# Attention beside a GELU layer on one core: the row maxima turned by VectorE's block transposition, their float16 parts made by GpSimd

## The chip, the cores and the metric

The kernel runs on one core of one Trainium2 chip. The core has five engines that run side by side, each with an instruction queue worked in order: TensorE (PE; PEld is its weight load), VectorE (DVE), ScalarE (ACT), GpSimd (POOL) and SyncE (SP). SP does no arithmetic here; it issues every transfer of the part that this text is about. TensorE writes its products to PSUM, eight banks of 128 partitions by 512 float32 numbers; the other memory of the core is SBUF. The metric is the device time of one execution in microseconds (us); less is better.

## The reference

One input x of 2048 rows and 512 columns goes through a layer normalization, and then through two branches whose results are added to x: attention with 32 heads of 16 numbers each, and a two-layer network with 1792 hidden numbers.

```python
def reference(A_x, A_wqkv, A_wo, B_x, B_w1, B_b1, B_w2, B_b2):
    def _A_ref(x, wqkv, wo):
        B, S, D = x.shape          # 1, 2048, 512
        H = 32
        Dh = D // H                # 16
        qkv = (lambda x, *d: x.transpose(*d))((x @ wqkv).reshape(B, S, 3, H, Dh), 2, 0, 3, 1, 4)
        q, k, v = qkv[0], qkv[1], qkv[2]
        scores = jnp.einsum("bhqd,bhkd->bhqk", q, k) * (Dh ** -0.5)
        p = _softmax(scores, axis=-1)
        o = jnp.einsum("bhqk,bhkd->bhqd", p, v)
        return (lambda x, *d: x.transpose(*d))(o, 0, 2, 1, 3).reshape(B, S, D) @ wo

    def _B_ref(x, w1, b1, w2, b2):
        h = _gelu(jnp.einsum("bsd,df->bsf", x, w1) + b1)
        return jnp.einsum("bsf,fd->bsd", h, w2) + b2

    x = A_x
    xn = _layernorm(x, axis=-1)
    return x + _A_ref(xn, A_wqkv, A_wo) + _B_ref(xn, B_w1, B_b1, B_w2, B_b2)
```

## The kernel before, in words

**Tiles and units.** Heads are taken in groups g of four (NG = 8), queries in blocks qb of 512 (NQB = 4). One group with one block is a tile t, 32 tiles in all. A tile has 16 units; a unit u = 16 t + i is 128 queries against 512 keys for the scores, and, later, 128 keys against 512 queries for the exponentials. So there are NU = 512 units.

**What a unit does.** The function `unit` writes out, for unit u, four score products (`s_half`, one for each head of the group): TensorE puts 128x512 scores into a bank pS, and VectorE takes their row maxima (`reduce_max`, line 259) into the tile mt. Between them stand the four exponentials (`e_half`) of unit e = u - 20 (LEAD = 20): TensorE computes the scores again, with keys on the partitions, into a bank pT, and ScalarE takes their exponentials into pe (line 304). After each two of these come products with the values (pV, `v_half`) of units e - 1 and e - 2, and some products of the dense work (pD: projections, the two-layer network), which fill TensorE. Nearly all products go through the helper at line 170, in four pieces of 32 columns.

**What becomes of the maxima.** The exponentials need the maximum of each query subtracted. That is done inside the product: the tiles kst and qst hold, for each head, 48 rows of float16 parts of keys and queries, and in rows 62 and 63 ones (kst) and the negative maxima (qst), as a high and a low float16 part. After unit 15 of a tile, `s_end` reduces mt to mneg (line 270, 128 queries in the partitions, 16 columns for head and query block, of 32 that the tile has). Then `store` turns mneg so that the queries lie along a row: TensorE multiplies it with the unit matrix into a bank pS (line 277, two products), VectorE makes the two parts mhl out of that bank (lines 280 and 281), SP writes mhl to the HBM tensor m_d (line 284, two transfers) and from there into rows 62 and 63 of the four heads of qst (line 289, four transfers, which wait until the writes have landed). The exponentials of that tile start with unit 20 after its first unit, which is the fifth unit (number 4, counted from 0) after the tile's last one.

**PSUM.** The banks are handed out in turn: three to scores (`banks("S")`), three to exponentials, one to the dense work, one to pV. A score product waits until VectorE has read the bank's last content, which is that of the score product three before it, or of `store`, which takes its bank from the same turn.

**Order.** All five engines follow the order in which the program is written out. `later(n, fn)` puts a function off by n ticks; `tick`, at the end of each unit, runs those that are due. `store` is put off by `later(1, ...)` from the end of the tile's last unit, so it is written out at the end of the next unit (number 0 of the next tile). GpSimd's larger steps wait in a list (`pooled`), of which each tick releases as many as fit an estimate of 2500 ns.

**Other steps that are named below.** `v_end` divides a tile's result by its sums: ScalarE copies it to osb, SP sends the sums through HBM (lines 342, 345, 352, 356), VectorE inverts them (dn, line 348), GpSimd multiplies and splits (osb and ot, lines 360 to 362). hh, t and g are stages of the GELU on GpSimd (lines 992 to 1022), xa and yt its summed result (lines 1033 to 1049), wc and xb weights and inputs that SP fetches (lines 565 and 560).

Of the kernel before, what the change touches and what calls it, by code (L numbers as in the profile page):

```python
# [8 lines left out]
F32 = mybir.dt.float32  # L9
F16 = mybir.dt.float16  # L10
I32 = mybir.dt.int32
AF = mybir.ActivationFunctionType
ALU = mybir.AluOpType
# [4 lines left out]
P = 128  # L18
S = 2048
# [24 lines left out]
MROW = 1024.0  # L44
# [4 lines left out]
def layer_kernel(ctx: ExitStack, tc: tile.TileContext, x, wqkv, wo, w1, b1, w2, b2, out):  # L49
    nc = tc.nc  # L50
# [3 lines left out]
    def pool(stack, name, bufs=1, space=None, side=None):  # L54
        kw = {k: v for k, v in (("space", space), ("side", side)) if v is not None}
        return stack.enter_context(tc.tile_pool(name=name, bufs=bufs, **kw))

    const = pool(ctx, "const")
    work = pool(ctx, "work")
# [9 lines left out]
    m_d = dram.tile([NG * NQB, 16, 2, P], F16, name="m_d")  # L69
# [4 lines left out]
    ident = const.tile([P, P], F32, name="ident")  # L74
# [30 lines left out]
    def bank_tile(k, tag):  # L105
        return ps.tile([P, QB], F32, tag=f"B{k}", bufs=1, name="p" + tag)

    def banks(tag):
        k = free_banks[tag].pop(0)
        free_banks[tag].append(k)  # L110
        return bank_tile(k, tag)
# [48 lines left out]
    def given(engine, ns):  # L160
        backlog[engine] += ns
# [32 lines left out]
    def tiled(user, dst, lhs, rhs, start, stop):  # L194

        for j in range(0, P, 32):
            product(user, dst[j:j + 32], lhs[:, j:j + 32], rhs, start=start, stop=stop)
# [15 lines left out]
    def later(n, fn, local=False):  # L213
        queue.append((slot[0] + n, fn, local))
# [25 lines left out]
    def flush():  # L240

        while steps or any(q[2] for q in queue):
            run_due()
            run_steps(True)
            slot[0] += 1

    def s_half(u, n):

        t, i = divmod(u, 16)
        g, qb = divmod(t, NQB)  # L250
        qt, kb = divmod(i, 4) if t else (i % 4, i // 4)
        if t not in mt_of:
            mt_of[t] = work.tile([P, 4, 4, 4], F32, name="mt", bufs=2)
        ks, qs = kst[g % 2], qst[g % 2]
        p, a = divmod(n, 2)
        r = slice(64 * a, 64 * a + 62)
        s = banks("S")
        tiled(None, s, qs[p][qb][r, qt * P:(qt + 1) * P], ks[p][kb][r, :], True, True)
        nc.vector.reduce_max(mt_of[t][:, n, qt, kb:kb + 1], s, axis=AX.X)  # L259
        given("dve", 600)  # L260

    def s_end(u):

        t, i = divmod(u, 16)
        if i < 15:
            return
        g, qb = divmod(t, NQB)
        qs = qst[g % 2]
        mneg = mnegs[t % 2]
        nc.vector.tensor_reduce(mneg[:, :16], mt_of[t].rearrange("p h t k -> p (h t) k"), axis=AX.X, op=ALU.max, negate=True)  # L270
        given("dve", 220)

        def store():

            pt = banks("S")
            for a in range(2):
                nc.tensor.matmul(pt[32 * a:32 * a + 32, :64], mneg[64 * a:64 * a + 64, :],
                                 ident[64 * a:64 * a + 64, 64 * a:64 * a + 64], start=True, stop=True)
            mhl = work.tile([64, 2, 64], F16, name="mhl", bufs=2)
            nc.vector.tensor_scalar_mul(mhl[:, 0], pt[:64, :64], 1.0 / MROW)  # L280
            nc.vector.scalar_tensor_tensor(mhl[:, 1], pt[:64, :64], 1.0 / MROW, mhl[:, 0], op0=ALU.mult, op1=ALU.subtract)
            given("dve", 300)
            for a in range(2):
                nc.sync.dma_start(m_d[t, :, :, 64 * a:64 * a + 64], mhl[32 * a:32 * a + 16])
            for p in range(2):
                for a in range(2):
                    h = 2 * p + a
                    dst = qs[p][qb][64 * a + 62:64 * a + 64, :].rearrange("r (t q) -> r t q", q=P)
                    nc.sync.dma_start(dst, m_d[t, 4 * h:4 * h + 4].rearrange("t r q -> r t q"))

        later(1, store)

    def e_half(u, n):

# [101 lines left out]
    NU = NG * NQB * 16  # L396
# [215 lines left out]
    def unit(gen):  # L612
# [7 lines left out]
        for a in range(2):  # L620
            for scores, n in ((0, 1), (1, 0), (1, 1), (0, 0)) if a == 0 else ((1, 2), (0, 3), (0, 2), (1, 3)):
                if scores and u < NU:
                    s_half(u, n)
                elif not scores and 0 <= e < NU:
                    e_half(e, n)
            if e >= 0:
                enter()

                w, r = (e - 2, 1) if a == 0 else (e - 1, 0)
                live = 0 <= w < NU  # L630
                new = r == 0 and w % 16 == 0
                dense(gen, 1 - r, lambda: v_half(w, r) if live and not new else None)
                if live and new:
                    v_half(w, r)

                for user, goes_on in (("V", live and not (r == 1 and w % 16 == 15)),
                                      ("D", cur[0] is not None and not cur[0].over())):
                    leave(user, goes_on)
                for k in backlog:
                    backlog[k] = max(0, backlog[k] - HALF)  # L640
                if live and r == 1:
                    v_end(w)
                ended()
        if u < NU:
            s_end(u)
# [12 lines left out]
    with ExitStack() as st1:  # L658
# [130 lines left out]
        def tile_and_unit(t):  # L789

            v = v_proj(t, wvh, vbank)
            for k in range(2):
                s_half(t, 2 * k)
                s_half(t, 2 * k + 1)
                some(v, 6)
            s_end(t)
            run(v)
# [409 lines left out]
```

## Time and profile before

| what | value |
|---|---|
| time, median of 3 runs (lowest to highest) | 1502.55 us (1499.8 to 1506.8) |
| the profiled execution: its own time, and its span | 1504.39 us, 1502.6 us |
| PE busy | 1471.0 us (98%) |
| DVE busy | 1374.5 us (91%) |
| ACT busy | 1231.7 us (82%) |
| POOL busy | 716.6 us (48%) |
| mean granted TensorE clock | 0.994 |

The span runs from the first to the last instruction that the profiler recorded; the execution's own time has some 1.8 us around it. A busy PE is not PE at its peak, since its instructions overlap: its 98% says that nearly always a product was under way, not that none could have come sooner. In a row of a timeline the first number is the start in us from the beginning of the span, the second the time from the first to the last of the instructions that the row puts together (xN says how many), and the square bracket, where there is one, the idle time before and what ended it.

### The profile page before, as it was taken

Reading aid. Unit: us, or ns where it says so; the run is one execution under the profiler, and the core shown is the slowest. Engines: PE = TensorE matmul, PEld = TensorE weight load, DVE = VectorE, ACT = ScalarE, POOL = GpSimd, SP = SyncE. Lnnn points to the kernel's source line nnn. Section 1 sums busy time; section 2 is a strip of 40 time slices with the busy share of each in tenths; the row PEclk is TensorE's granted clock in tenths of the full one; section 3 lists DMA queues with packets and bytes.
Section 4 is the critical chain, followed back from the end, with each engine's and each line's share of the span. In section 5 each row is a group of like instructions: output and inputs, shape, how many; then the busy total and the mean of one; then the engine's idle time right before and its main releaser. Section 6 shows DMA issues by size and latency. Waiting matters only on the chain.

```text
span 1502.6 us, 87920 instructions
## 1 busy us (share of the span) xinstructions
PE 1471.0 (98%) x39971; PEld 931.1 (62%) x39971; DVE 1374.5 (91%) x2372; ACT 1231.7 (82%) x2326; POOL 716.6 (48%) x750
## 2 busy tenths in 40 slices
PE   8998999999999999999999999999999999999997
PEld 4434566666666666666666666666666666666653
DVE  7898989999999999999999999999999999999612
ACT  5315878899999889989998998998899999988771
POOL 4113597547665545537553554665264465511000
PEclk9999999999999999999999999999999999999998
DMA  6454476633211311121112211121112111022412
GB/s 207 129 172 139 160 217 221 196 116 94 71 37 44 89 43 37 36 68 54 36 51 59 63 37 37 35 83 57 37 43 63 53 32 35 23 68 81 152 35 89
DMA packets 113677, 123.82 MB, mean 82 GB/s; under 512 B 24988, under 2 KB 85276, under 8 KB 113304
## 3 DMA queue, kind: packets, MB, share of 16 engines
q1 hardware_dynamic: 113304, 118.21, 25.5%
q8 instruction: 312, 5.11, 1.4%
q14 instruction: 61, 0.50, 0.1%
HBM read 80.61 MB, written 37.34 MB: 78 GB/s over the span
## 4 chain that ended last, share of the span: by engine, by line
PE 81%; DVE 13%; DMA 2%; issue 2%; SPq 1%; ACT 1%; POOL 0%; ACTq 0%; POOLq 0%
PE pV L170 22%; PE pD L170 20%; PE pS L170 19%; PE pT L170 17%; DVE mt L259 11%; PE pT L444 1%; PE pS L444 1%; DVE amx L679 1%; PE pT L543 1%; PE pD L444 1%; DMA m_d<-mhl 1%; PE pV L543 0%; SPq L1080 0%; DMA xs<-in_A_x_dram 0%; DVE mneg L270 0%
## 5 line engine op out<-in xcount | busy, mean ns | idle before, releaser
L259 DVE TENSOR_REDUCE mt<-pS 128x1 f32<-128x512 f32 x2048 | 1274.3, 683 | 37.4 <-PE pS L170 22.4
L304 ACT ACTIVATE pe<-pT 128x512 f32<-128x512 f32 x2048 | 1107.0, 600 | 153.3 <-PE pT L170 79.2
L170 PE MATMUL pV<-pe,vv 64*32 64x512 f32 x8192 | 1093.1, 599 | 1.1 <-issue 1.0
L170 PE MATMUL pT<-qst,kst 64*32 64x512 f16 x8192 | 668.5, 377 | 3.5 <-ACT pe L304 1.8
L170 PE MATMUL pS<-kst,qst 62*32 62x512 f16 x8192 | 632.7, 379 | 8.7 <-DVE mt L259 6.1
L170 PE MATMUL pD<-xb,wc 64*32 64x512 f16 x5376 | 372.1, 375 | 0.0
L170 PE MATMUL pD<-w_s,g 64*32 64x512 f16 (+1 forms) x6144 | 362.0, 348 | 0.0
L170 PEld LDWEIGHTS <-qst 62*32 62x32 f16 x8192 | 248.1, 92 | 140.6 <-issue 49.5
L170 PEld LDWEIGHTS <-kst 64*32 64x32 f16 x8192 | 251.8, 93 | 101.4 <-issue 13.9
L170 PEld LDWEIGHTS <-g 64*32 64x32 f16 x6144 | 196.1, 92 | 85.3 <-issue 0.7
L170 PEld LDWEIGHTS <-wc 64*32 64x32 f16 x5376 | 177.4, 91 | 98.4
L170 PEld LDWEIGHTS pV<-pe,vv 64*32 64x32 f32 x8192 | 172.5, 105 | 6.0 <-issue 2.2
L1022 POOL TENSOR_SCALAR hh<-hh,fac,b_s 128x512 f32<-128x512 f32 x56 | 43.0, 768 | 265.3 <-ACT hh L1020 265.3
L170 PE MATMUL pD<-xt,wqk_h 64*32 64x512 f16 x1920 | 129.8, 377 | 3.1 <-issue 3.0
L360 POOL TENSOR_TENSOR osb<-osb,rb 128x512 f32<-128x512 f32 x31 | 39.8, 1283 | 140.1 <-DMA rb<-den_d 101.9
L1049 POOL TENSOR_TENSOR xa<-xa,yt 128x512 f32<-128x512 f32 x32 | 41.1, 1283 | 108.4 <-ACT yt L1047 108.4
L170 PEld LDWEIGHTS <-wqk_h 64*32 64x32 f16 x1920 | 61.8, 92 | 27.7 <-issue 3.6
L1086 DVE SCALAR_TENSOR_TENSOR ac<-pS,gs,ac 128x512 f32<-128x512 f32 x20 | 15.0, 751 | 66.1 <-PE pS L170 57.2
L993 POOL TENSOR_TENSOR t<-t,hh 128x512 f32<-128x512 f32 x56 | 71.8, 1283 | 4.7
L1000 POOL TENSOR_TENSOR t<-t,hh 128x512 f32<-128x512 f32 x56 | 71.7, 1281 | 4.7
L995 POOL TENSOR_TENSOR g<-t,g 128x512 f16<-128x512 f32 x56 | 65.2, 1164 | 4.7
L170 PE MATMUL pS<-wo_s,oc 64*32 64x512 f16 x1008 | 62.6, 377 | 0.4
(140 smaller groups left out, 926.3 us busy)
## 6 DMA issues: line engine op xcount, KB each, us to landing
wch<-in_B_w_dram SPq DMA_DIRECT2D x28, 512.0 KB
wc<-w_d SPq DMA_DIRECT2D x56, 256.0 KB
qk_d<-stg SPq DMA_DIRECT2D x32, 256.0 KB
rb<-den_d SPq DMA_DIRECT2D x124, 64.0 KB
w_d<-wsp SPq DMA_DIRECT2D x28, 256.0 KB
kst<-qk_d SPq DMA_DIRECT2D x128, 48.0 KB
qst<-qk_d SPq DMA_DIRECT2D x128, 48.0 KB
xs<-in_A_x_dram SPq DMA_DIRECT2D x16, 256.0 KB
```

Source lines behind the costliest of these rows:

```text
L170: p = nc.tensor.matmul(*args, **kw)
L259: nc.vector.reduce_max(mt_of[t][:, n, qt, kb:kb + 1], s, axis=AX.X)
L304: nc.scalar.activation(pe, st, AF.Exp, scale=factor(exp_scale, sexp[0:1, g // 2:g // 2 + 1]))
L360: pooled((1280, lambda: nc.gpsimd.tensor_tensor(osb, osb, rb, op=ALU.mult)), (620, lambda: nc.gpsimd.tensor_scalar(ot[:, 0], osb, 1.0, 0.0 ...
L444: nc.tensor.matmul(self.bank, lhs, rhs, start=start, stop=self.last and self.over())
L543: nc.tensor.matmul(pj, xt[:, i, c, t * P:(t + 1) * P], wh[j][:, c, :], start=(n == 0), stop=(n == 11))
L679: nc.vector.tensor_reduce(dst, v, axis=AX.XY if len(v.shape) == 3 else AX.X, op=ALU.max, apply_absolute_value=True)
L993: (1280, lambda: nc.gpsimd.tensor_tensor(t1, t1, hh, op=ALU.mult)),
L995: (1160, lambda: nc.gpsimd.tensor_tensor(g[:, 1, f, :], t1, g[:, 0, f, :], op=ALU.subtract)),
L1000: (1280, lambda: nc.gpsimd.tensor_tensor(t1, t1, hh, op=ALU.mult)),
L1022: later(1, lambda: pooled((690, lambda: nc.gpsimd.tensor_scalar(hh, hh, scale, bias, op0=ALU.mult, op1=ALU.add)), (0, lambda: gelu(hh, g, ...
L1049: add = lambda: nc.gpsimd.tensor_tensor(xa, xa, yt, op=ALU.add)
```

## The change

The transposition on TensorE goes, and with it the bank that it took and VectorE's two instructions that read this bank. In their place, VectorE transposes mneg in blocks of 32x32, in SBUF, into a new tile mrow of 128x32 (so block a holds queries 32 a to 32 a + 31, its rows 0 to 15 the head and query block). This is written out inside the next unit, right after that unit's first maximum; for the last tile at once. GpSimd then scales mrow in place and makes the two parts of mhl, in three instructions that stand outside the `pooled` list. SP writes mhl in four transfers (16 partitions x 2 parts x 32 numbers each) instead of two (16 x 2 x 64); the four transfers into qst are as before.

```diff
+    rows = []
     def s_half(u, n):
...
         nc.vector.reduce_max(mt_of[t][:, n, qt, kb:kb + 1], s, axis=AX.X)
         given("dve", 600)
+        if rows:
+            rows.pop()()
 
     def s_end(u):
...
+        pt = work.tile([P, 32], F32, name="mrow", bufs=2)
         def store():
-            pt = banks("S")
-            for a in range(2):
-                nc.tensor.matmul(pt[32 * a:32 * a + 32, :64], mneg[64 * a:64 * a + 64, :],
-                                 ident[64 * a:64 * a + 64, 64 * a:64 * a + 64], start=True, stop=True)
-            mhl = work.tile([64, 2, 64], F16, name="mhl", bufs=2)
-            nc.vector.tensor_scalar_mul(mhl[:, 0], pt[:64, :64], 1.0 / MROW)
-            nc.vector.scalar_tensor_tensor(mhl[:, 1], pt[:64, :64], 1.0 / MROW, mhl[:, 0], op0=ALU.mult, op1=ALU.subtract)
-            given("dve", 300)
-            for a in range(2):
-                nc.sync.dma_start(m_d[t, :, :, 64 * a:64 * a + 64], mhl[32 * a:32 * a + 16])
+            nc.vector.transpose(pt, mneg)
+            given("dve", 130)
+            mhl = work.tile([P, 2, 32], F16, name="mhl", bufs=2)
+            nc.gpsimd.tensor_scalar(pt, pt, 1.0 / MROW, 0.0, op0=ALU.mult, op1=ALU.add)
+            nc.gpsimd.tensor_scalar(mhl[:, 0], pt, 1.0, 0.0, op0=ALU.mult, op1=ALU.add)
+            nc.gpsimd.tensor_tensor(mhl[:, 1], pt, mhl[:, 0], op=ALU.subtract)
+            later(0, lambda: put(mhl))
+
+        def put(mhl):
+            for a in range(4):
+                nc.sync.dma_start(m_d[t, :, :, 32 * a:32 * a + 32], mhl[32 * a:32 * a + 16])
...
-        later(1, store)
+        rows.append(store)
+        if u == NU - 1:
+            rows.pop()()
```

How the instructions move is shown at the end of one tile in the middle of the program (tile 14 for PE and DVE). On PE, in the order at the beginning of unit 1 of the next tile (the difference; pT is a bank for exponentials, pD one of the dense work):

```order
 L170 LDWEIGHTS wc
 L170 MATMUL pD<-xb,wc 32x512
-L277 MATMUL pS<-ident,mneg_118 32x64 x2
 L170 LDWEIGHTS kst_0_3_92
 L170 MATMUL pT<-qst_0_1_106,kst_0_3_92 32x512
```

The two products with the unit matrix are gone; nothing else moved there.

On DVE, before, from the last maxima of tile 14 on (a trailing xN counts equal rows; the next tile's RECIPROCAL belongs to `v_end`):

```order
L259 TENSOR_REDUCE mt<-pS 128x1 [waits PE_49] x16
L270 TENSOR_REDUCE mneg_118<-mt 128x16 [waits DVE_49]
L259 TENSOR_REDUCE mt<-pS 128x1 [waits PE_49] x4
L280 TENSOR_SCALAR mhl<-pS 64x64 [waits DMAHW2_49,PE_49]
L281 SCALAR_TENSOR_TENSOR mhl<-pS,mhl 64x64 [waits DVE_49]
L259 TENSOR_REDUCE mt<-pS 128x1 [waits PE_49] x44
L348 RECIPROCAL dn<-dn 64x32 [waits DMAHW3_49,DMAHW1_49]
```

and now (the lines of the changed file are some ten higher):

```order
L261 TENSOR_REDUCE mt<-pS 128x1 [waits PE_49] x16
L274 TENSOR_REDUCE mneg_118<-mt 128x16 [waits DVE_49]
L261 TENSOR_REDUCE mt<-pS 128x1 [waits PE_49]
L281 STREAM_TRANSPOSE mrow<-mneg_118 128x32 [waits DVE_49,Pool_49]
L261 TENSOR_REDUCE mt<-pS 128x1 [waits PE_49] x47
L357 RECIPROCAL dn<-dn 64x32 [waits DMAHW7_49]
```

Two instructions after the fourth maximum of unit 0 became one after the first, and it no longer waits for PE.

On SP, at the end of tile 6, before:

```order
L356 DMA rb<-den_d 32x512 [waits DMAHW5_49]
L284 DMA m_d<-mhl 32x1x64 [waits DMAHW6_49,DVE_49]
L284 DMA m_d<-mhl 32x1x64
L289 DMA qst_0_2_107<-m_d 2x4x128 [waits DMAHW7_49,DMAHW6_49,DMAHW0_49]
L289 DMA qst_0_2_107<-m_d 2x4x128 [waits DMAHW1_49]
```

and now:

```order
L365 DMA rb<-den_d 32x512 [waits DMAHW1_49]
L291 DMA m_d<-mhl 32x1x32 [waits DMAHW2_49,Pool_49]
L291 DMA m_d<-mhl 32x1x32
L291 DMA m_d<-mhl 32x1x32 [waits DMAHW4_49]
L291 DMA m_d<-mhl 32x1x32 [waits DMAHW5_49]
L296 DMA qst_0_2_107<-m_d 2x4x128 [waits DMAHW5_49,DMAHW4_49,DMAHW6_49,DMAHW3_49,DMAHW2_49]
```

The writes stand at the same place among SP's transfers as before (behind the same rb), four now, waiting for GpSimd instead of VectorE; the reads wait for all four. Only for the first and the last tile are they written out one unit sooner: there `store` used to fall one tick later.

## Prediction

> **What bounds the kernel now.** I read the page first: the busy shares, then the chain of work that ended last, then the costliest groups.
>
> ```profile
> span 1502.6 us, 87920 instructions
> PE 1471.0 (98%) x39971; PEld 931.1 (62%) x39971; DVE 1374.5 (91%) x2372; ACT 1231.7 (82%) x2326; POOL 716.6 (48%) x750
> PE 81%; DVE 13%; DMA 2%; issue 2%; SPq 1%; ACT 1%; POOL 0%; ACTq 0%; POOLq 0%
> L259 DVE TENSOR_REDUCE mt<-pS 128x1 f32<-128x512 f32 x2048 | 1274.3, 683 | 37.4 <-PE pS L170 22.4
> ```
>
> PE carries 81% of the chain and the row maxima on DVE 13%. POOL has half its time free and 0% of the chain. So what counts is how fast PE gets through its units, and where DVE holds it up. The groups of instructions show no such hold-up, because a wait of a few tenths of a us inside overlapping products is not idle time. I therefore read the timeline of PE around one end of a tile (tile 14, whose maxima end at 713.56), keeping the rows of score products and of the transposition:
>
> ```profile
> 712.99 0.44 PE L170 MATMUL pS<-kst,qst 62*32 62x512 f16 x8
> ...
> 715.33 0.39 PE L170 MATMUL pT<-qst,kst 64*32 64x512 f16 x3
> 715.35 0.27 PE L277 MATMUL pS<-ident,mneg 64*32 64x64 f32 x2
> ...
> 715.51 0.27 PE L277 MATMUL pS<-ident,mneg 64*32 64x64 f32 x2
> 715.62 0.40 PE L170 MATMUL pS<-kst,qst 62*32 62x512 f16 x4
> 716.22 0.40 PE L170 MATMUL pS<-kst,qst 62*32 62x512 f16 x4 [0.20 <-DVE mt L259]
> ...
> 718.57 0.43 PE L170 MATMUL pS<-kst,qst 62*32 62x512 f16 x8
> ...
> 743.82 0.54 PE L170 MATMUL pS<-kst,qst 62*32 62x512 f16 x8
> ...
> 748.85 0.44 PE L170 MATMUL pS<-kst,qst 62*32 62x512 f16 x8
> ...
> 753.87 0.45 PE L170 MATMUL pS<-kst,qst 62*32 62x512 f16 x8
> ```
>
> Units begin at 712.99 (unit 0 of tile 15), 715.62 (unit 1), 718.57 (unit 2) and, fourteen units later, at 753.87. A plain unit takes (753.87 - 718.57) / 14 = 2.52 us. Unit 1 takes 2.95, so 0.43 more. One sees why: in a plain unit the first two score products form one row of eight; in unit 1 the second comes 0.60 us after the first, held by DVE. The transposition has taken a bank out of the turn, so this score product needs the bank whose maximum DVE is only just reading. DVE at the same place:
>
> ```profile
> 713.56 0.22 DVE L270 TENSOR_REDUCE mneg<-mt 128x16 f32<-128x64 f32 x1
> 713.70 2.48 DVE L259 TENSOR_REDUCE mt<-pS 128x1 f32<-128x512 f32 x4
> 716.09 0.21 DVE L280 TENSOR_SCALAR mhl<-pS 64x64 f16<-64x64 f32 x1
> 716.33 0.22 DVE L281 SCALAR_TENSOR_TENSOR mhl<-pS,mhl 64x64 f16<-64x64 f32 x1
> 716.47 2.54 DVE L259 TENSOR_REDUCE mt<-pS 128x1 f32<-128x512 f32 x4
> ...
> 744.16 0.33 DVE L348 RECIPROCAL dn<-dn 64x32 f32<-64x32 f32 x1
> 744.42 3.17 DVE L259 TENSOR_REDUCE mt<-pS 128x1 f32<-128x512 f32 x5
> ```
>
> The four maxima of a unit take DVE from 713.70 to 716.09, 2.39 us, so of a unit of 2.52 it has 0.13 to spare. mneg costs it 0.14 and the two parts of mhl 716.47 - 716.09 = 0.38. That tile 14 is no exception, the distance of tile ends shows:
>
> ```profile
> L270 DVE TENSOR_REDUCE mneg<-mt x27: 219/220/221, 302.4 to 1369.3; 128x16 f32<-128x64 f32 x27
> ```
>
> 26 tiles in 1066.9 us are 41.03 each; 16 plain units would be 40.3. Unit 1's 0.43 is more than half of the difference.
>
> **The change part by part.** *PE and the bank.* Two products a tile go, and the bank with them; the second score product of unit 1 then needs a bank that DVE left one maximum (0.60 us) earlier. Taken alone that gives back 0.43 us a tile.
>
> *VectorE.* 0.38 us go, a transposition of 128x32 float32 comes. No such instruction is in the trace. Its bounds are the time from start to next start of the smallest and of the dearest small instruction on SBUF:
>
> ```profile
> 35.00 0.15 DVE L728 SCALAR_TENSOR_TENSOR sd<-sd 128x4 f32<-128x4 f32 x1
> 35.12 0.18 DVE L715 BATCH_NORM_AGGREGATE mv<-bs 128x2 f32<-128x6 f32 x1
> ```
>
> These are 0.12 below and 0.26 (the reciprocal, 744.16 to 744.42) above; I take 0.14, near the lower, as mneg reads twice as many numbers in 0.14. The Trainium skill (VectorE: DVE Perf Modes, The three transpose paths) gives 311 ns for a 128x128 bf16 transposition on this engine; as an estimate a quarter of the columns would be some 80 ns plus a fixed part, and the sum would be the same to 0.04 us a tile. It stands between the first and the second maximum of unit 0, where DVE is already 0.14 late from mneg. Does this delay reach PE? The reciprocal is the test: 0.26 us put in at 744.16, and the two units from 743.82 to 748.85 take 5.03 us, 2.515 each, so nothing reached PE. At a tile's end, mneg and the transposition make 0.28, just beyond that. In tile 14 DVE came to its end with no gap, so the third maximum would end at about 715.72 instead of 715.58 (713.70 plus two steps of 0.60 plus 0.68), while PE would want the bank at about 715.55. The delay that reaches PE lies between 0 (the reciprocal's case) and 0.29 (0.03 that it has there anyhow plus 0.26); I take 0.08, nearer to the reciprocal's case. So 0.35 us a tile is gained.
>
> *GpSimd.* Three instructions of 128x32 come. Durations at 512 and 1024 columns give their price:
>
> ```profile
> L909 POOL TENSOR_TENSOR wsp<-wch,wsp 128x1024 f16<-128x1024 f32 x14 | 30.0, 2143 | 1.1
> L995 POOL TENSOR_TENSOR g<-t,g 128x512 f16<-128x512 f32 x56 | 65.2, 1164 | 4.7
> ...
> L994 POOL TENSOR_SCALAR g<-t 128x512 f16<-128x512 f32 x56 | 34.6, 618 | 4.9
> L908 POOL TENSOR_SCALAR wsp<-wch 128x1024 f16<-128x1024 f32 x14 | 14.6, 1045 | 1.2
> ```
>
> Straight lines through them give 0.22 us at 32 columns for one input and 0.25 for two: 0.69 in all, with hand-overs about 0.75; at 48% busy this is covered. GpSimd works in order, so the steps behind wait for the transposition too, up to some 5 us where GpSimd was ahead. That hits mostly osb and ot, which SP sends six ticks (15 us) after they are written out; I cost it at nothing, and without that cover SP would stall behind ot.
>
> *The transfers.* Ready time after mneg's start: 0.14 + 0.60 + 0.14 + 0.75, about 1.65, say 1.75 with hand-overs; where GpSimd is busy, later. Two views bound this and the way on (GpSimd, then SP and PE at the ends of tiles 14, 9 and 13, then the wait of SP ahead of the reads):
>
> ```profile
> 384.56 0.22 DVE L270 TENSOR_REDUCE mneg<-mt 128x16 f32<-128x64 f32 x1
> ...
> 386.72 1.27 POOL L1033 TENSOR_TENSOR xa<-xa,b_b 128x512 f32<-128x512 f32 x1
> ...
> 716.57 1.22 SPq L284 DMA_DIRECT2D m_d<-mhl  x2
> 719.65 1.16 SPq L289 DMA_DIRECT2D qst<-m_d  x4
> 723.40 0.40 PE L170 MATMUL pT<-qst,kst 64*32 64x512 f16 x4
> ...
> 512.05 1.22 SPq L284 DMA_DIRECT2D m_d<-mhl  x2
> 517.00 1.16 SPq L289 DMA_DIRECT2D qst<-m_d  x4
> 518.62 0.40 PE L170 MATMUL pT<-qst,kst 64*32 64x512 f16 x4 [1.18 <-DMA qst<-m_d]
> ...
> 676.54 1.21 SPq L284 DMA_DIRECT2D m_d<-mhl  x2
> 680.70 1.15 SPq L289 DMA_DIRECT2D qst<-m_d  x4
> 682.35 0.40 PE L170 MATMUL pT<-qst,kst 64*32 64x512 f16 x4
> ...
> L289 SPq EVENT_SEMAPHORE  x32: 17/1127/3647, 118.2 to 1417.6; - x32
> ```
>
> At 384.56 GpSimd's next slot came 2.16 us after mneg's start; the latest that I found at any tile's end, so the parts are ready by 2.9 there, against 3.01 (716.57 - 713.56) before. Each write costs SP 0.61, so four take 2.44 instead of 1.22; then SP waits for them to land, 1.13 as the median and 3.65 at most. The reads thus start 1.75 + 2.44 + 1.13 = 5.3 us after mneg as a rule. When must they? PE reaches unit 4's exponentials 9.84 us after mneg (723.40), 0.35 less after the change; at 518.62 PE went on 0.46 after the reads' row ended. So the reads must start by 9.49 - 0.46 - 1.16 = 7.87. There are 2.5 us to spare, and nothing is lost as a rule.
>
> Exceptions are the tiles where SP came late to the writes for another reason. At tile 9 (512.05, behind big fetches) PE waited 1.18 or more already; the reads are held by what is queued there, so they do not move and the gain of 0.4 is lost. At tile 13 the reads started just about in time; two writes more put them 0 to 1.2 later, so 0.4 to 1.6 is lost, of which I take 0.5. Together 0.9.
>
> *The sum.* 27 tile ends from 302.4 on at 0.35 are 9.45. The first four lie where units are longer and PE is not always full: half, 0.7. The last costs PE only the 0.27 of the products. 9.45 + 0.7 + 0.27 - 0.9 = 9.5 us. The profiled execution took 1504.39 (span 1502.6), so it would take 1494.9; the median of the runs shown, 1502.55, becomes 1493.0.
>
> **The rivals.** *First, the hold-up stays in part.* DVE runs without gaps into the tile's end, and mneg and the transposition now stand close together; if most of the 0.29 reaches PE, 0.14 a tile is left: 3.8 + 0.3 + 0.27 - 0.9, about 3.5, so 1499. For it speaks that DVE has only 0.13 a unit to catch up; against it the reciprocal. Chance 0.2.
>
> *Second, slower: PE waits for the reads at every tile.* This decides once the reads start later than 7.87 after mneg. They would if the small writes took not 1.13 but over 3.7 us to land, which only the worst case of 3.65 comes near. To lose 9.5 and 8 more, each of 32 waits must be 0.55 us, so 4.2 us for landing: 1510. In a sentence of its own, the Trainium skill (DMA: Bandwidth & Descriptors, Specifications) says that transfers under 512 B are written by read-modify-write, which speaks against cutting m_d's rows from 128 to 64 B. No run here shows rows of 64 B; by twice the landing time the reads would start at 6.5, still in time, so this alone does not bring it about. Chance 0.07.
>
> *Third, the whole gain.* The transposition hides like the reciprocal and the exceptions cost nothing: 27 x 0.43 + 4 x 0.43 + 0.3 = 13.6, so 1489. Chance 0.07.
>
> *Fourth, the words don't hold.* The order of SP shows the transfers sooner by a unit only for the first and last tile; what comes sooner elsewhere is the data. If early data were the point, nothing would come of it, since PE waited for these reads at two or three tiles only. The time then hangs on the first two terms alone, as in the sum. If these were covered by ScalarE (82% busy), no change, 1502. Chance 0.05.
>
> **How the numbers follow.** Forecast (a gain of 7.5 to 13) 0.61, first rival 0.2, second 0.07, third 0.07, fourth 0.05. About 0.5%, 7.5 us, is what a measurement of this kernel can tell from no change: below 1495 is faster. Forecast and third make 0.68 faster; the first and the fourth 0.25 the same; the second 0.07 slower. The range reaches from the third (1489, with half a us for the spread of runs) to the first, 1500.
>
> **What would show it.** Right: unit 1 of a tile lasts about 2.6 us and its first two score products make one row; mneg's distance falls from 41.03 to about 40.7; the transposition takes about 0.14; the writes start 1.8 to 2.9 us after mneg; only one to three waits of PE for qst. Wrong: a row of pS in unit 0 or 1 that waits for the maxima, or PE waiting for qst at most tiles.

## The result, and the profile after

The median of 16 runs is 1495.27 us (1490.65 to 1503.26), against 1506.09 us (1499.8 to 1511.74) for 16 runs of the kernel before on the same chips: 10.8 us less, a ratio of 0.9936 with a 95% interval of 0.9918 to 0.9955. The profiled execution took 1492.57 us.

The page after: span, busy time, the chain of work that ended last, and the costliest group.

```profile
span 1490.8 us, 87790 instructions
PE 1456.4 (98%) x39843; PEld 928.4 (62%) x39843; DVE 1364.1 (92%) x2340; ACT 1229.9 (82%) x2326; POOL 739.9 (50%) x846
PE 86%; DVE 4%; DMA 3%; POOL 2%; SPq 1%; issue 1%; ACT 1%; POOLq 0%
L261 DVE TENSOR_REDUCE mt<-pS 128x1 f32<-128x512 f32 x2048 | 1270.3, 682 | 38.2 <-PE pS L170 23.8
```

Nearly nothing changed in the busy shares, yet DVE fell from 13% to 4% of the chain, and PE rose from 81% to 86%. DMA stands on it with 3% (2% before), of which the transfers of the maxima into m_d and into qst make 1% each, and POOL with 2% (0%), mainly GpSimd's work ahead of the parts at the ends of tiles 6 (361.8 to 381.8 us) and 8 (459.0 to 462.9). What that costs is shown below. The end of tile 14 again, PE's timeline first (the rows with which units 0, 1 and 2 of tile 15 begin):

```profile
705.85 0.44 PE L170 MATMUL pS<-kst,qst 62*32 62x512 f16 x8
...
708.36 0.61 PE L170 MATMUL pS<-kst,qst 62*32 62x512 f16 x8
...
710.93 0.44 PE L170 MATMUL pS<-kst,qst 62*32 62x512 f16 x8
```

Unit 0 lasts 708.36 - 705.85 = 2.51 us and unit 1 710.93 - 708.36 = 2.57 (before: 2.63 and 2.95). In unit 1 the first two score products make one row of eight again. DVE, POOL and SP at the same place, from their timelines:

```profile
706.42 0.22 DVE L274 TENSOR_REDUCE mneg<-mt 128x16 f32<-128x64 f32 x1
706.55 0.68 DVE L261 TENSOR_REDUCE mt<-pS 128x1 f32<-128x512 f32 x1
707.15 0.20 DVE L281 STREAM_TRANSPOSE mrow<-mneg 128x32 f32<-128x32 f32 x1
707.28 2.44 DVE L261 TENSOR_REDUCE mt<-pS 128x1 f32<-128x512 f32 x4
```

```profile
707.44 0.22 POOL L284 TENSOR_SCALAR mrow<-mrow 128x32 f32<-128x32 f32 x1 [1.96 <-DVE mrow L281]
707.74 0.22 POOL L285 TENSOR_SCALAR mhl<-mrow 128x32 f16<-128x32 f32 x1
708.05 0.25 POOL L286 TENSOR_TENSOR mhl<-mrow,mhl 128x32 f16<-128x32 f32 x1
```

```profile
708.32 2.50 SPq L291 DMA_DIRECT2D m_d<-mhl  x4
711.99 1.15 SPq L296 DMA_DIRECT2D qst<-m_d  x4
```

The transposition costs DVE 707.28 - 707.15 = 0.13 us. The writes start 1.90 after mneg (706.42), the reads 5.57. Over the same 27 tile ends as before:

```profile
L274 DVE TENSOR_REDUCE mneg<-mt x27: 220/220/222, 297.0 to 1354.9; 128x16 f32<-128x64 f32 x27
L281 DVE STREAM_TRANSPOSE mrow<-mneg x27: 201/202/203, 297.7 to 1355.6; 128x32 f32<-128x32 f32 x27
```

(1354.9 - 297.0) / 26 = 40.69 us a tile, before 41.03. What got worse is in the list of waits, the kernel before first, then after:

```profile
PEld L170 <- DMA qst<-m_d: 2.8, 2, 2.1
PE pT L170 <- DMA qst<-m_d: 1.2, 1, 1.2
```

```profile
PEld L170 <- DMA qst<-m_d: 8.2, 6, 2.6
PE pT L170 <- DMA qst<-m_d: 4.8, 4, 2.0
```

The columns are us in total, times, and the longest. The weight load (PEld) and PE wait at the same products, so the two lines of a list don't add up to more waits: the maxima's way through HBM now holds the weight load at six tile ends instead of two, and PE itself at four of these instead of one.

### The profile page after: what moved, and what is told of

The parts are those of the page before. It is cut to its first block, busy times and chain, and to the rows that moved or that the text cites. A ratio compares the mean times of both kernels' runs of the same rounds, so it can differ in the third digit from the quotient of the medians.

```text
span 1490.8 us, 87790 instructions
## 1 busy us (share of the span) xinstructions
PE 1456.4 (98%) x39843; PEld 928.4 (62%) x39843; DVE 1364.1 (92%) x2340; ACT 1229.9 (82%) x2326; POOL 739.9 (50%) x846
## 4 chain that ended last, share of the span: by engine, by line
PE 86%; DVE 4%; DMA 3%; POOL 2%; SPq 1%; issue 1%; ACT 1%; POOLq 0%
PE pV L170 23%; PE pD L170 21%; PE pS L170 20%; PE pT L170 18%; DVE mt L261 2%; PE pT L453 1%; PE pS L453 1%; DMA m_d<-mhl 1%; DVE amx L688 1%; SPq L291 1%; PE pT L552 1%; PE pD L453 1%; DMA qst<-m_d 1%; DMA ac<-acc_d 0%; PE pV L552 0%
## 5 line engine op out<-in xcount | busy, mean ns | idle before, releaser
L170 PE MATMUL pS<-kst,qst 62*32 62x512 f16 x8192 | 619.7, 378 | 6.1 <-DVE mt L261 5.9
L170 PEld LDWEIGHTS pV<-pe,vv 64*32 64x32 f32 x8192 | 169.1, 105 | 4.3 <-issue 1.0
```

The source lines that it names most:

```text
L170: p = nc.tensor.matmul(*args, **kw)
```

## The experiments

A measure for all of them: from the trace I took the lengths of the 16 units of tiles 5 to 29 (start of a unit's first score product to that of the next) and added up what units 0 to 2 and units 3 to 5 of these 25 tiles lasted above the lengths they have when nothing holds them (2.54, 2.49, 2.54; 2.51, 2.54, 2.57). The first sum is the hold-up at the tile's end. The second is mostly waits for qst, which strike at unit 3 or 4, and at one tile end a wait for GpSimd (see e5). All of it comes from one profiled execution of each kernel; the ratio to the kernel before comes from all of its runs.

| kernel | median us | ratio (95% interval) | units 0-2 over, us | units 3-5 over, us |
|---|---|---|---|---|
| before | 1506.09 to 1509.58 | 1 | 12.0 | 2.3 |
| after | 1495.27 | 0.9936 (0.9918 to 0.9955) | 0.0 | 6.4 |
| e10_after_again | 1500.56 | 0.9955 (0.9932 to 0.9979) | 0.1 | 12.4 |
| e1_skip_bank | 1511.24 | 1.0014 (1.0003 to 1.0025) | 13.9 | 3.3 |
| e2_pe_only | 1503.55 | 0.9970 (0.9952 to 0.9988) | 1.0 | 10.8 |
| e3_parts_on_dve | 1542.34 | 1.0222 (1.0199 to 1.0244) | 45.1 | 1.0 |
| e4_two_writes | 1491.98 | 0.9889 (0.9873 to 0.9906) | 0.3 | 2.3 |
| e11_two_writes_again | 1489.48 | 0.9868 (0.9839 to 0.9897) | 0.0 | 7.0 |
| e5_pool_writes | 1493.09 | 0.9903 (0.9886 to 0.9919) | 0.4 | 3.6 |
| e6_dve_load | 1506.36 | 0.9983 (0.9970 to 0.9997) | 14.8 | 1.0 |
| e7_turn_at_once | 1495.95 | 0.9917 (0.9901 to 0.9934) | 4.6 | 1.6 |
| e8_dve_scalar | 1508.48 | 1.0001 (0.9986 to 1.0016) | 17.9 | 0.1 |
| e9_load_late | 1495.58 | 0.9915 (0.9890 to 0.9939) | 5.1 | 1.7 |

In e1 to e3 the base is the changed kernel. e4 to e9 and e11 stand on the version with two writes.

**The bank alone (e1).** In the changed kernel one bank of the scores' turn is passed over at each tile end, as the transposition on TensorE had done, and nothing is put into it.

```diff
+            if 0 < t < NG * NQB - 1:
+                later(0, lambda: free_banks["S"].append(free_banks["S"].pop(0)))
```

> The changed kernel, but one bank of the scores' turn is passed over, unused, where the old transposition took one (for tiles 1 to 30). No product of the transposition and no VectorE instruction comes back. Theory A (the 0.43 us of unit 1 came from the bank taken out of the turn): unit 1 goes from 2.51 back to about 2.9 us, the distance of tile ends from 40.69 to about 41.05, and the time to about that of the kernel before (ratio 0.997 to 1.002). Rival B (TensorE's own time in the transposing products, 0.27 us) and rival C (VectorE's relief, 0.38 us of instructions less): unit 1 stays at 2.5, ratio stays at 0.994.

Measured: 1.0014; the whole gain is gone, and more. Units 0 and 1 last 2.63 and 2.95 us in the median. PE at the beginning of unit 1 of such a tile (keeping the score products), and the wait of the whole run, which counted 7 times and 5.9 us in the changed kernel:

```profile
716.12 0.40 PE L170 MATMUL pS<-kst,qst 62*32 62x512 f16 x4
716.72 0.40 PE L170 MATMUL pS<-kst,qst 62*32 62x512 f16 x4 [0.20 <-DVE mt L261]
```

```profile
PE pS L170 <- DVE mt L261: 10.7, 36, 0.9
```

The second score product again stands 0.60 after the first, with no product of the unit matrix and without the two instructions on mhl on DVE. So taking the bank out of the turn suffices to bring the old hold-up. The edit leaves out the end of tile 0, so it says nothing about tile 1.

**The products alone (e2).** The two products of the old size are put back on TensorE, into the bank that unit 1's first score product is to overwrite, so the turn keeps its banks.

```diff
+        if t > 0 and i == 1 and n == 0:
+            for b in range(2):
+                nc.tensor.matmul(s[32 * b:32 * b + 32, :64], mnegs[(t - 1) % 2][:64, :],
+                                 ident[:64, :64], start=True, stop=True)
```

> The changed kernel, with two products of the size of the old transposition put back on TensorE at the start of unit 1, written into the bank that the next score product overwrites, so that no bank is taken and VectorE reads nothing more. Theory A: unit 1 grows by at most the 0.27 us that these products stood for in the trace of before, rather less since they wait for nothing: 0.1, and ratio 0.994 to 0.996. Rival B: unit 1 grows by 0.27 us or more, 8 us in all, ratio 0.999. Rival C: no growth.

Measured: 1.0 us over in units 0 to 2 of 25 tiles, 0.04 a tile. TensorE's own time for the transposition was nearly free there. The ratio of 0.997, above the 0.994 to 0.996 that was expected, is not explained by that. Between the profiled executions of e2 and of the changed kernel run again (e10) lie 6.4 us: units 0 to 2 make 0.9 of them, units 3 to 5 are 1.6 shorter in e2, and tiles 1 to 4 are 3.8 longer. Whether the products cost something in tiles 1 to 4, or these differ from one execution to the next, isn't shown; the intervals of the two ratios overlap.

**The parts on VectorE (e3).** The three instructions that make the parts go from GpSimd to VectorE, right behind the transposition.

```diff
-            nc.gpsimd.tensor_scalar(pt, pt, 1.0 / MROW, 0.0, op0=ALU.mult, op1=ALU.add)
-            nc.gpsimd.tensor_scalar(mhl[:, 0], pt, 1.0, 0.0, op0=ALU.mult, op1=ALU.add)
-            nc.gpsimd.tensor_tensor(mhl[:, 1], pt, mhl[:, 0], op=ALU.subtract)
+            nc.vector.tensor_scalar(pt, pt, 1.0 / MROW, 0.0, op0=ALU.mult, op1=ALU.add)
+            nc.vector.tensor_scalar(mhl[:, 0], pt, 1.0, 0.0, op0=ALU.mult, op1=ALU.add)
+            nc.vector.tensor_tensor(mhl[:, 1], pt, mhl[:, 0], op=ALU.subtract)
```

> The changed kernel, with the three small instructions that make the float16 parts on VectorE instead of GpSimd. VectorE then has mneg 0.14, the transposition about 0.13 and the parts about 0.4 us (estimate from 0.12 to 0.26 from start to start of small instructions) within one unit, against 0.14 and 0.38 before the change. Theory A: the bank's turn stays whole, but some 0.5 us of delay is beyond the 0.28 that stayed hidden, so 0.1 to 0.3 us a tile reach TensorE: ratio 0.996 to 0.999. Rival C (what counts is VectorE's load): slower than before by 0.1 to 0.2 us a tile, ratio 1.002 to 1.005. Should the load not matter at all, 0.994.

Measured: 1.0222, 2.2% slower than before, and far beyond what any of the theories allowed (1.005). Unit 0 lasts 3.73 us in the median. Most of the reason stands in the timelines of DVE and of POOL at one tile's end:

```profile
726.17 0.20 DVE L281 STREAM_TRANSPOSE mrow<-mneg 128x32 f32<-128x32 f32 x1
726.41 0.18 DVE L284 TENSOR_SCALAR mrow<-mrow 128x32 f32<-128x32 f32 x1
726.62 1.11 DVE L285 TENSOR_SCALAR mhl<-mrow 128x32 f16<-128x32 f32 x1
727.76 0.19 DVE L286 TENSOR_TENSOR mhl<-mrow,mhl 128x32 f16<-128x32 f32 x1
```

```profile
725.83 0.62 POOL L370 TENSOR_SCALAR ot<-osb 128x512 f16<-128x512 f32 x1
726.53 1.16 POOL L371 TENSOR_TENSOR ot<-osb,ot 128x512 f16<-128x512 f32 x1
```

L285 lasts 1.11 us, and ends (727.73) just after GpSimd's instruction (727.69) that was under way when it started. The next one, of the same size, takes 0.19. Over all tiles (lowest, median, highest, in ns):

```profile
L285 DVE TENSOR_SCALAR mhl<-mrow x32: 180/182/1207, 108.5 to 1448.3; 128x32 f16<-128x32 f32 x32
L286 DVE TENSOR_TENSOR mhl<-mrow,mhl x32: 191/193/1199, 108.7 to 1448.5; 128x32 f16<-128x32 f32 x32
```

At 14 of the 25 tile ends at least one of the three instructions stood still like this. At the other 11, units 0 and 1 last 2.71 and 2.95 us in the median, 0.6 us a tile more than in the changed kernel, so part of the loss is the load alone.

The Trainium skill (SBUF — State Buffer, Who interferes with whom) says that GpSimd and a VectorE instruction in a two-port mode, which a tensor_scalar can enter, block one another for the whole instruction, that a VectorE instruction with two inputs in SBUF contends with a GpSimd instruction that reads SBUF, and that on trn2 a tensor_reduce never does. The rows fit all three: 1207 and 1199 ns at most here, and mneg (a tensor_reduce) never over 222 ns, though at 19 of e3's 32 tile ends it ran wholly inside one GpSimd instruction. In which mode L285 ran, no row shows. In the kernel before, L281 had one of its inputs in the PSUM bank and was never held up:

```profile
L281 DVE SCALAR_TENSOR_TENSOR mhl<-pS,mhl x27: 216/217/218, 305.2 to 1372.1; 64x64 f16<-64x64 f32 x27
```

**Two writes (e4, again as e11), and the changed kernel again (e10).** m_d gets 32 rows, so that one transfer writes all 128 partitions of a part, rows that nobody reads included: two writes instead of four, still in pieces of 64 bytes.

```diff
-    m_d = dram.tile([NG * NQB, 16, 2, P], F16, name="m_d")
+    m_d = dram.tile([NG * NQB, 32, 2, P], F16, name="m_d")
-            for a in range(4):
-                nc.sync.dma_start(m_d[t, :, :, 32 * a:32 * a + 32], mhl[32 * a:32 * a + 16])
+            for i in range(2):
+                nc.sync.dma_start(m_d[t, :, i].rearrange("r (c q) -> c r q", q=32), mhl[:, i])
```

> The changed kernel, with the maxima written by two transfers (one for the high, one for the low parts of all 128 partitions, twice as many rows of 64 B, half of them zeros) instead of four. SP issues the reads 1.2 us sooner. Theory D (four writes on SP are what makes TensorE wait 13 us for qst in the changed kernel's profile, against 4 before): the waits fall to 3 to 6 us, and the time by some 4 to 8 us against the changed kernel: ratio 0.989 to 0.992. Rival E (these waits come from the transfers queued in front of the writes): waits stay at 10 us or more, ratio 0.994.

Measured: 0.9889, better than the changed kernel, as theory D has it. SP at the end of tile 14, whose mneg starts at 703.51:

```profile
705.08 1.26 SPq L291 DMA_DIRECT2D m_d<-mhl  x2
707.78 1.16 SPq L296 DMA_DIRECT2D qst<-m_d  x4
```

From the first write to the first read it is 2.70 us, against 3.67 with four writes (711.99 - 708.32). Over tiles 5 to 29 the medians are 2.71 against 4.59, and the reads start 4.4 us after mneg instead of 7.2. No wait of PE for qst is left in the list of waits of e4.

Because that part of the time depends on how late SP is in a given execution, I ran both once more, side by side.

> The changed kernel as it is, on the same chip as the next one, for comparison: ratio 0.992 to 0.996 to the kernel before, and PE's waits for qst 8 us or more in all, if they belong to the four writes and not to the one execution that was profiled.

> The kernel with two writes once more, on the same chip as the changed kernel: ratio 0.987 to 0.991, 0.3 to 0.6% below the changed kernel, no waits of PE for qst of more than 3 us in all. Rival: 0.2% or less between the two, if the difference was the chip's or the day's.

Measured: 1500.56 and 1489.48 us, 0.74% apart, more than the 0.3 to 0.6% expected. In the profiled execution of e10 the waits for qst are longer than in that of the same kernel above:

```profile
PEld L170 <- DMA qst<-m_d: 13.8, 9, 2.8
PE pT L170 <- DMA qst<-m_d: 8.6, 7, 2.1
```

Five ends of tiles 5 to 29 had reads more than 7.9 us after mneg (tiles 5, 6, 9, 13 and 25), against four in the changed kernel's profile and none in e4. Two writes are no full cure: in e11, at tile 9, SP came to the writes 6.9 us after mneg, and the next tile, in which PE then waited, lasted 44.8 us, where others last 40.4. In all, PE waited 3.2 us for qst in e11, a little more than the 3 that were allowed. All the same, e11's times (1485.81 to 1492.23) lie below all of e10's (1493.03 to 1512.53). Of the kernels tried, the one with two writes is the fastest.

**Writes on GpSimd's queue (e5).** As e4, but GpSimd issues the two writes.

```diff
-                nc.sync.dma_start(m_d[t, :, i].rearrange("r (c q) -> c r q", q=32), mhl[:, i])
+                nc.gpsimd.dma_start(m_d[t, :, i].rearrange("r (c q) -> c r q", q=32), mhl[:, i])
```

> The kernel with two writes, with these writes issued by GpSimd from its own queue instead of by SP. Theory E (what was queued on SP ahead of the writes made TensorE wait for qst at tiles 5, 9 and 25 of the changed kernel): nothing on SP is in front of them any more, but with two writes there are no waits for qst left in the profile, so the time stays (ratio 0.988 to 0.990). Rival H: GpSimd's own issuing takes about 1 us or more a write and puts the steps behind it off, or the transfers land later from this queue; reads start later than 4.2 us after mneg, ratio 0.991 or more.

Measured: 0.9903, the same as e4 within the intervals. The reads start 4.6 to 7.4 us after mneg, in the median of the tile ends 0.66 later than in e4, and the weight load waits for qst at two tile ends, 0.6 us at most. SP's queue is thus not the only way; taking the writes off it brings nothing more.

What it costs instead is a wait for GpSimd, which the change itself had brought. At the end of tile 6 the three instructions on the parts stand between two steps of the GELU, and PE needs the second step's result g in unit 4 of tile 7. The waits for g there, before and in e4:

```profile
PEld L170 <- POOL g L995: 0.4, 1, 0.4
```

```profile
PEld L170 <- POOL g L1004: 1.1, 1, 1.1
PEld L170 <- POOL g L1003: 0.8, 1, 0.8
```

In e4 the three hold GpSimd's next step back by 0.80 us (380.62 to 381.42), and that unit lasts 3.67 us, against 2.47 before; PE also comes there 0.4 us sooner, since unit 1 is no longer held up. In e5 the two writes take 1.40 us more of GpSimd at this place, and it lasts 5.14; that is the greater part of e5's 3.6 us in units 3 to 5.

**How much VectorE can bear (e6, e7, e8, e9).** In e6 three idle maxima stand right behind the transposition; in e8 three idle tensor_scalar of 128x32 instead; in e7 the transposition stands directly behind mneg; in e9 two idle maxima stand behind unit 0's fourth maximum, where the kernel before had its two instructions on mhl.

```diff
 e6, right behind the transposition:
+            for k in range(3):
+                nc.vector.tensor_reduce(spare[:, :16], spare[:, 16:].rearrange("p (a b) -> p a b", b=4), axis=AX.X, op=ALU.max)
 e8, at the same place:
+            for k in range(3):
+                nc.vector.tensor_scalar(spare[:, :32], spare[:, 32:], 1.0, 0.0, op0=ALU.mult, op1=ALU.add)
 e9, put off by later(0, ...):
+            for k in range(2 if t < NG * NQB - 1 else 0):
+                nc.vector.tensor_reduce(spare[:, :16], spare[:, 16:].rearrange("p (a b) -> p a b", b=4), axis=AX.X, op=ALU.max)
 e7, at the end of s_end instead of behind the next maximum:
+        nc.vector.transpose(pt, mneg)
```

> The kernel with two writes, plus three idle instructions on VectorE right behind the transposition: maxima of 128x64 numbers in SBUF into an unused tile, of the kind and size of mneg (0.14 us each from start to start, 0.42 in all). They read one operand in SBUF. Theory F (in the run with the parts on VectorE, its instructions stood still while GpSimd was inside an instruction; load alone is cheap): each takes 0.22 us always, unit 0 and 1 together grow by at most 0.42, ratio 0.990 to 0.997. Rival G (three more instructions of any kind at this place cost the 1.6 us a tile that were measured there): ratio 1.01 or more.

> The kernel with two writes, with the transposition directly behind mneg instead of one maximum later. It has to wait for mneg to land, so VectorE idles for some 0.1 us (estimate: mneg lasts 0.22, and the next maximum used to start 0.14 after it), and mneg and the transposition come before the first maximum of the next tile. If the place behind the first maximum is worth something, unit 1 grows by 0.05 to 0.15 us, ratio 0.990 to 0.992; the writes start 0.5 us sooner after mneg. If not, ratio 0.989 and the units stay.

> The kernel with two writes, plus three idle tensor_scalar instructions on VectorE at the same place, 128x32 float32 from SBUF to SBUF in an unused tile; the parts stay on GpSimd. Theory F: the instructions take 0.18 us where GpSimd is between instructions, and up to 1.2 us where it is inside one; now the parts on GpSimd themselves (0.22 to 0.25 us) stand in the way as well. Unit 0 grows by 1 us or more at about half of the tiles: ratio 1.00 to 1.015. Rival G: the same as the three maxima, within 0.002 of their ratio.

> The kernel with two writes, plus two idle maxima of 128x64 numbers on VectorE after the fourth maximum of unit 0, where the kernel before had its two instructions that read the transposed bank; no bank is taken and TensorE gets nothing. VectorE then has, around a tile's end, about as much to do as before the change (mneg 0.14, transposition 0.13, these two 0.3 to 0.4, against 0.14 and 0.38). Theory A (the bank out of turn alone made unit 1 long): units 0 and 1 grow by 0.1 at most, ratio 0.989 to 0.991. Theory A2 (VectorE's delay alone makes unit 1 long as well, as the three idle maxima did that stood earlier): unit 1 at 2.9 again, ratio 0.996 to 0.999; then both had to go, the bank and the instructions.

Measured, e6: unit 1 lasts 2.95 us again and the ratio is 0.9983, with all banks in the turn. That lies between the two theories: 0.6 us a tile, where F allowed 0.42 and G had 1.6. So the bank suffices, but is not the only thing that suffices: DVE, late enough, holds the same score product. Its wait in the list:

```profile
PE pS L172 <- DVE mt L263: 10.0, 35, 0.9
```

e8 does the same, with 17.9 us in units 0 to 2 against 14.8: at five of the 25 tile ends one of its instructions stood still behind GpSimd's (182 ns in the median, 1043 at most). F had expected that at half of them, but at 17 of the 25 no GpSimd instruction of over 0.4 us was under way then. The ratio of 1.0001 fits F (1.00 or more) and G (within 0.002 of e6) alike; what speaks for F is how long single instructions lasted. One tile's end from its timelines of DVE and POOL:

```profile
589.30 0.20 DVE L283 STREAM_TRANSPOSE mrow<-mneg 128x32 f32<-128x32 f32 x1
589.42 1.52 DVE L286 TENSOR_SCALAR spare<-spare 128x32 f32<-128x32 f32 x3
```

```profile
589.14 1.29 POOL L1013 TENSOR_TENSOR t<-t,hh 128x512 f32<-128x512 f32 x1
```

The three last 1.52 us here, while the transposition, with the same GpSimd instruction under way, takes its 0.20. e7 costs 4.6 us in 25 tiles, 0.18 a tile, because the transposition has to wait for mneg to be written (it starts 0.33 after mneg's start, and the next maximum 0.46 after it). e9 shows the load at its old place, in DVE's timeline:

```profile
704.36 1.84 DVE L263 TENSOR_REDUCE mt<-pS 128x1 f32<-128x512 f32 x3
706.12 0.46 DVE L294 TENSOR_REDUCE spare<-spare 128x16 f32<-128x64 f32 x2
706.50 0.68 DVE L263 TENSOR_REDUCE mt<-pS 128x1 f32<-128x512 f32 x1
```

706.50 - 706.12 is 0.38, as much as mhl's instructions had cost. It brings 5.1 us in 25 tiles, spread over units 1 and 2 (2.58 and 2.63 in the median), where the kernel before lost 12.0 and e1 13.9. So of the old 0.48 a tile, VectorE's load alone makes at most 0.20 (e9 also holds the transposition, 0.13, which the kernel before had not), and the bank alone all of it, 0.56 in e1; the two together cost no more than the bank. The ratio of e9, 0.9915, lies just beyond theory A's 0.991 and far from A2's 0.996.

How thin the margin is, the bank shows: in the changed kernel the second score product of unit 1 starts 54 ns after the end of the maximum that read its bank, as the median over tiles 5 to 29, and 119 ns at most; in e6, where this product has to wait, it is 53 ns. So it comes just in time, or waits for next to nothing.

## Why the prediction was right, and where it was not

**Unit 1 and the bank: right.** Unit 1 went from 2.94 to 2.51 us as a median of tiles 5 to 29, its first two score products make one row in the tile end shown, and e1 shows the bank as a sufficient cause.

**VectorE's delay: rightly bounded, sized too high.** The transposition took 0.13 against 0.14 taken (its whole duration is 0.20; the Trainium skill, VectorE: DVE Perf Modes, The three transpose paths, has 311 ns for a 128x128 in bf16, a size that no run here shows). Of the 0.08 that was to reach PE, nothing did: units 0 to 2 lost 0.0 us. The gain there was 12.0 / 25 = 0.48 a tile instead of 0.35. The first rival, that the hold-up stays, lacked little: in e7 the maxima of unit 0 start 0.46 us after mneg instead of 0.14 with another 0.13 behind the first, 0.19 more, and this already cost 0.18 a tile.

**GpSimd: the price right, the cost not nothing.** 0.22, 0.22 and 0.25 us, as read off the lines. Its busy time rose by 23 us, and units 6 to 15 of the 25 tiles stayed at 631 us (631.9 before, 631.3 after). The delay of the steps behind, "I cost it at nothing", does reach PE at the end of tile 6: in e4, where the reads are in time, unit 4 of tile 7 is 1.2 us longer than before, waiting for g (see e5). And at the ends of tiles 6 and 8 GpSimd's own steps delay the parts, as the chain of work shows. PE waited for g there, not for osb and ot, on which the prediction had its eye.

**The transfers: wrong in size.** The step that failed is "the reads thus start 1.75 + 2.44 + 1.13 = 5.3 us after mneg as a rule", and with it "there are 2.5 us to spare" and the 0.9 us for exceptions. Terms of the usual case were added up, and each of them often takes longer. As means over tiles 5 to 29, which may be added, the first write comes 2.51 us after mneg (1.75 predicted; the median is 1.90), the four writes take 2.95 (2.44), and from the end of the last write's issue to the reads it is 1.72 (1.13; the median is 1.29): 7.2 instead of 5.3. The kernel before already showed the last of these, 1.79 as a mean and 1.30 as a median, and its first write came at 3.23 as a mean where 3.01 was the rule. Four writes were often pulled apart, 3.7 us from first to last end at the end of tile 26 against the 2.50 of tile 14:

```profile
1194.32 3.70 SPq L291 DMA_DIRECT2D m_d<-mhl  x4
1199.19 1.15 SPq L296 DMA_DIRECT2D qst<-m_d  x4
```

So the reads start 7.2 us after mneg, in the median too. The limit of 7.87 was about right: at tile 17, with 7.89, nothing was lost, at tile 6, with 8.51, PE stood 0.80, but at tile 8 7.29 already cost 0.2. With 0.7 us to spare instead of 2.5, four tile ends are late in the changed kernel's profile, as at tile 9 (SP, then PE at unit 4's exponentials):

```profile
507.34 3.37 SPq L291 DMA_DIRECT2D m_d<-mhl  x4
511.87 1.15 SPq L296 DMA_DIRECT2D qst<-m_d  x4
```

```profile
513.67 0.40 PE L170 MATMUL pT<-qst,kst 64*32 64x512 f16 x4 [2.02 <-DMA qst<-m_d]
```

At these four (tiles 5, 6, 9 and 25) everything came together: the first write came 3.2 to 5.6 us after mneg, and from there to the reads it was 4.5 to 6.0. Units 3 to 5 lost 6.4 - 2.3 = 4.1 us more than before in this profile, and 10.1 more in e10's, against 0.9 predicted. Not all of it would have been saved by reads in time: at tile 6 the wait for g stands behind the wait for qst, and e4 lost as much there. "Only one to three waits of PE for qst" was wrong: PE waited at four tile ends, its weight load at six. The writes did not start "1.8 to 2.9 us after mneg" at six of the 25 tile ends, but later. The second rival had the right place with the wrong reason, and at some tiles only. The rows of 64 bytes did not land later: from the end of the last write's issue to the reads it is 1.29 us in the median and 1.17 at least with them, 1.30 and 1.20 with rows of 128 bytes before. What the number of writes costs, e4 shows: two take 1.25 us instead of 2.95, and the reads start 4.9 us after mneg as a mean instead of 7.2. The rule of the Trainium skill (DMA: Bandwidth & Descriptors, Specifications) on transfers under 512 B, which stood beside this rival, had no cost in cutting rows from 128 to 64 bytes that these runs show.

**The sum.** Between the two profiled executions lie 11.8 us, against 9.5 predicted, 10.8 between the medians, and the terms missed in both directions. Tiles 5 to 29 gave 8.5 (25 x 0.35 - 0.9 = 7.9 predicted): 0.13 more a tile, 3.2 more waiting, and 0.6 in units 6 to 15. Tiles 1 to 4 gave 5.2 instead of 0.7. Of these, 1.6 come from tile 1, where DVE is behind and held PE at the beginning of unit 2 in the kernel before:

```profile
116.38 0.40 PE L170 MATMUL pS<-kst,qst 62*32 62x512 f16 x4 [0.35 <-DVE mhl L281]
118.16 0.40 PE L170 MATMUL pS<-kst,qst 62*32 62x512 f16 x4 [1.39 <-DVE mt L259]
```

That unit lasted 5.66 us there and 4.22 after. It lasts 4.22 in e1 too, which leaves the bank in the turn at this place, so whether the bank or DVE's two instructions made it long isn't shown. The other 3.6 come from tiles 2 to 4, and their cause stays open: these lasted 139.7 us before and 136.1 after, 140.3 in e1, but also 141.1 in e2, whose turn has all its banks, while the other kernels with a whole turn, without e3, have 134.8 to 137.9. In each of these profiles PE stands there for 3.2 to 6.1 us without a wait that the profile shows ("issue"). From tile 30 to the last unit the profile of the changed kernel lost 1.9 us, in e10 it gained 0.6; what makes that differ was not looked into. That the time fits is thus partly luck. The 0.13 a tile that the hold-up gave more and the 4.5 us of tiles 1 to 4 made up for waits that were taken too small and for what the end of the program lost. Nor do 1493.0 and the measured 1495.27 compare directly: the first was worked out from 1502.55, the median of 3 runs, where 16 runs of the kernel before have 1506.09.

**The fourth rival** was half right: as medians, the transfers are sooner by 1.1 us at their start (1.90 against 3.01 after mneg), and later where it counts, at the reads (7.2 against 6.1). In tiles 5 to 29 the gain came from the bank and from DVE's load.

## What to carry to other kernels

Here, where VectorE had 0.13 us a unit to spare, a bank lent out of a turn for one small step cost more (0.56 us a tile in e1) than the work in it (0.04 in e2, at most 0.20 in e9). So look at which product needs the buffer next and when its last reader comes. When a transfer is cut into more, count the issue of each and the whole stretch from the first write to the dependent read as it lasted before, and don't add up the usual values where the late cases are what costs. When small steps go to an engine that works in order, look for the step behind them that somebody waits for. And before small work is moved onto VectorE in SBUF, look at what GpSimd runs at that moment.

## What the runs showed of the hardware

A tensor_scalar of 128x32 on VectorE, 0.18 us by itself, lasted up to 1.2 us while GpSimd was inside one instruction (e3; 1.04 in e8). The block transposition, also from SBUF to SBUF, never stood still: 201 to 203 ns at 27 tile ends of the changed kernel, and in e3 202 ns at most at the 14 tile ends where it ran wholly inside one GpSimd instruction. The same kernel can differ by 19 us from run to run (e10, 1493.03 to 1512.53) at a clock between 0.989 and 0.995. In its profiled execution units 3 to 5 last 10.1 us more than before, nearly all of it at five tile ends whose reads came late; whether such waits make the spread of all its runs was not tried.
